# Attention beside a token MLP: score banks as two groups of three, VectorE's tiles in a group's last bank, the schedule's table replaced

## Chip, cores and metric

One core of one Trainium2 chip runs the whole program. The metric is the device time in microseconds (us) of one execution; lower is better. Runs of the kernel before: 757.68, 756.87, 756.53 and 756.96 us, median 756.91.

## What is computed

The input x has 2048 tokens of 640 features. A layer norm feeds two branches, and their product is added to x.

```python
xn = _layernorm(x)                       # (1, 2048, 640)
# branch A: 32 heads of 20 features, all 2048 keys, then wo
scores = einsum("bhqd,bhkd->bhqk", q, k) * (20 ** -0.5)
o = einsum("bhqk,bhkd->bhqd", softmax(scores), v)
s = merge_heads(o) @ wo
# branch B: an MLP over the tokens, on a layer norm of xn
u = gelu(einsum("bsd,sf->bdf", h, w1) + b1)      # w1 2048x1536
g = silu(einsum("bdf,fs->bds", u, w2) + b2)      # w2 1536x2048
out = x + s * g
```

The costly part is the softmax: 32 x 2048 x 2048 exponentials.

## The kernel before, in words

**Units.** Heads are taken in 8 groups of four, queries in 4 blocks of 512: 32 passes. In a pass there are 16 chunks of 128 keys and four heads, so 64 units (pass, chunk, head): a unit is one score tile of 128 keys by 512 queries, one PSUM bank of 512 floats, 2048 units in all. The four heads of a group sit in the four 32-row groups of TensorE (PE), so score matmuls of different heads run side by side (`emit_st`, the matmul of L1212).

**Two engines make exponentials.** ScalarE (ACT) takes neighbouring banks in one instruction (`emit_exp`, L1241): an exp of two units (128x1024, a "pair") or of three (128x1536, a "triple"), written to `pt_sb`. VectorE (DVE) takes its units by a bit trick: one instruction per unit from PSUM to 16-bit integers (`emit_op1`, L1252, tiles `dt_sb`), and three instructions per four units that add constants (`emit_top`, L1276). The four results are combined in the following matmuls with scaled values. DVE's units come from five chunks in a pass (`RC`), at most; the planner decides as it goes. Then the PV matmuls (`pv_mm`, L1292) multiply by the values and accumulate a pass in bank 6 (`AB`), and DVE finishes the pass (L1408 and after).

**Banks.** PSUM has eight. ACT's units go to `ACT_GROUPS = ((0, 1, 2), (3, 4))`, taken in turn: while ACT reads one group, PE fills the other. Bank 5 (`DB`) holds a unit for DVE and nothing else, once the start is over; bank 6 is the accumulator; bank 7 (`JB`) serves every other job that needs a bank (projections, MLP) and, when free, DVE (`SHARE`). A group of three may *lend* its last bank: the set of score matmuls then gives ACT a pair and DVE the third bank (`do_st`). That is done when DVE has less than `LEND` ns of work waiting in the planner's account.

**Other work.** The projections, the values, both MLP halves (L645) and the output projection (L930) are PE jobs put between the sets; their evacuations are on DVE, some at the start on ACT (L1044, L1047). All DMAs are issued by SyncE (SP) in one order. Weights of the MLP come in parts of 1 MB and 768 KB, two parts at a time in `regA` (L775, L782).

**What sets the order.** `schedule` is a planner that runs while the program is built: it holds a clock per engine and a cost per instruction, picks the next instruction, and so writes a fixed order for each engine, with semaphore waits where data or banks cross engines. Its options are switched every 16 units by a table, `PLAN`: a row has one digit for each entry of `OPTS` and picks one of that option's values (`tune`). The start, in which the layer norm, the transposes and the first projections feed the first passes, is called ramp in the code; in it all free banks serve jobs until the first score tile is due (`withdraw`). A job that holds a bank of a group keeps the group from being filled (`fin_bank`). At the end the banks of the score ring become `tbank`, in which the output projection of the last four token blocks is begun before the last pass is done (`tail_pre`).

Of the kernel before, what the change touches and what calls it, by code (L numbers as in the profile page):

```python
# [260 lines left out]
class _Kern:  # L261
# [4 lines left out]
    NG = 8  # L266
    EPS = 1e-5
    RP = 20
    ACT_GROUPS = ((0, 1, 2), (3, 4))
    DB = 5  # L270
    AB = 6
    JB = 7
    RC = (2, 5, 8, 11, 14)
# [12 lines left out]
    CONFL = True  # L286
    FILL, FGAP, FACT = True, 40.0, 0.6
    LATE = 2.0
    LEND, LEND_MIN = 1100.0, 3
    SHARE = True  # L290
    VPRIO = 24.0
    QAT = (0.0, 0.0, 0.0, 0.0)
# [10 lines left out]
        ("MINJ", (640.0, 320.0, 1000.0)),  # L303
        ("ROOM", (3, 6, 0)),
        ("DRIDE", (400.0, 150.0, 700.0)),
        ("LEND", (900.0, 300.0, 1500.0, 0.0, 2500.0)),
        ("PARTS", ((2,), (2, 1), (3, 1), (1,), ())),
        ("LATE", (2.0, -9.0, 99.0)),
        ("DON", (True, False)),
# [5 lines left out]
        ("GROT", (1, 0)),  # L315
    )
    PLAN = (
        "00000000000010", "00000000000000", "00000000000010", "00000000000000", "00000410000000", "10010410000100",
        "00004010011000", "20204010111000", "00000000000000", "02000020010010", "00000000000000", "00000010001000",
        "00000000000000", "01000120000000", "01003120000000", "00000000000000", "00000010000100", "00000310100000",  # L320
        "02020320011000", "02020320011000", "02120010011000", "00000220000100", "30000220000100", "02000010000000",
        "00000000000000", "00000000100000", "02000100100100", "01000120001010", "00000000000000", "00003300000000",
        "00000000000000", "01000000000010", "00004000000000", "10011000000000", "01022300000000", "00000000000000",
        "30020100000000", "02000010110000", "00000100000000", "00010100000110", "00001000000000", "20100000000100",
        "11000000000000", "00000000000000", "00001000010000", "10020000000000", "10020000010000", "10020010010000",
        "00000000000000", "22103000000000", "22103010000000", "01220100000100", "00000000000000", "00100000001000",
        "02000000100000", "01000300001000", "01000300001000", "00000000000000", "00100000001000", "00100400100000",
        "01000000001000", "00004000000000", "10002000010000", "01001400001010", "01021420000110", "00000300000000",
        "00000020000010", "00000000000000", "00000010001000", "10000100000000", "10000100000000", "10004100001000",
        "00004120000000", "00001010000000", "10011410000110", "11001200000110", "11001200100110", "00020000000000",  # L330
        "00000000000000", "00000000100100", "00200400100000", "02100010110010", "02101010100010", "01000000000000",
        "01000000000000", "00000000000000", "00000400000000", "00000000000000", "00000020001000", "00020320000000",
        "00000000000000", "01000010000000", "01000010000100", "20000000000100", "02000000000000", "12000000000000",
        "00001000101000", "00000000000000", "00200000010100", "00020020100000", "01003000000000", "22000000000000",
        "21210000000000", "00000000000000", "00200020110000", "00000000000000", "00200000000100", "00000000001000",
        "00020310000100", "00220020000010", "10224000000010", "31223410000010", "30200000000100", "00021000000010",
        "00100000001010", "01100000010010", "01204001000000", "01204100001000", "00204100000010", "02024120000000",
        "02024320000000", "02000200000000", "12000200010000", "00000000000000", "00001000100000", "00001000100000",
        "00000000001000", "10000000000000", "00000000000000",
    )  # L340
    PARTS = (2,)
    DX = (1, 2, 3)
# [74 lines left out]
    def schedule(self):  # L417
        pr, t, nc = self.prog, self.t, self.nc
        S, NB, NTB, F, FC, D, H, DH, NG, GH = (self.S, self.NB, self.NTB, self.F, self.FC, self.D,
                                               self.H, self.DH, self.NG, self.GH)  # L420
# [11 lines left out]
        PROW = 4096  # L432
        A_x, A_wqkv, A_wo, B_w1, B_b1, B_w2, B_b2, out = (self.A_x, self.A_wqkv, self.A_wo, self.B_w1,
                                                          self.B_b1, self.B_w2, self.B_b2, self.out)
        AB, DB, JB = self.AB, self.DB, self.JB
        RC, NR = self.RC, len(self.RC)
        sl = {}

# [11 lines left out]
        done = set()  # L450
# [320 lines left out]
        def dma_w1(k):  # L771
            src = B_w1[:, k * 256:(k + 1) * 256].rearrange("(b p) f -> p b f", p=P)
            dst = w1_ap(k)
            wr = [S_(f"wm{k % 2}")]
            return ("dma", lambda e: e.dma_start(dst, src), [], wr, f"dma_w1_{k}", S * 512,  # L775
                    [S_(f"x{b}") for b in range(NB)] if k < 2 else [])

        def dma_w2(k):
            src = B_w2[:, k * 256:(k + 1) * 256].rearrange("(fc p) s -> p fc s", p=P)
            dst = w2_ap(k)  # L780
            wr = [S_(f"wn{k % 2}")]
            return ("dma", lambda e: e.dma_start(dst, src), [], wr, f"dma_w2_{k}", F * 512,  # L782
                    [S_("wm0"), S_("wm1")] if k < 2 else [])

        def ztmp(i):
# [181 lines left out]

        jobs = []
        bankq = []
        freebanks = [3, 4, DB, 0, 1, 2, JB]  # L970
        retired = set()
        busybanks = set()
        active = []
# [85 lines left out]
        dquads = []  # L1059
        tfree = list(range(self.NTILE))  # L1060
        dlive = [0]
        dbank = ["free"]
        dop1 = []
        lent = set()
        dtop = []
# [97 lines left out]
        def d_bank():  # L1163
            if not dveready[0]:
                return None
            if DB in bank_off:
                return None
            if dbank[0] == "free" and fin_bank(DB):
                return DB
            if self.SHARE and JB in freebanks and len(dop1) < 2 and not ramp[0]:  # L1170
                return JB
            return None

        def d_take(g, bk):
            d = d_cur[0]
            if d is None:
                q, c, r = d_claimable()
                claimed.add((q, c))
                dlive[0] += 1
                d = d_cur[0] = dict(q=q, c=c, r=r, todo=[0, 1, 2, 3], tl=[tfree.pop(0), None, None, None], fin=[0.0] * 4, left=4, pk=0)  # L1180
                stats["dve_units"] += 4
                nd_pass[q] += 1
            d["todo"].remove(g)
            if bk == DB:
                dbank[0] = "full"
            elif bk == JB:
                freebanks.remove(bk)
                busybanks.add(bk)
            else:
                lent.add(bk)  # L1190
            dop1.append((d, g, bk))
            u = (d["q"], d["c"], g)
            if not d["todo"]:
                d_cur[0] = None
            return u
# [52 lines left out]
        def emit_op1():  # L1248
            d, g, bk = dop1.pop(0)
            w = dt_sb[:, d["tl"][0], g, :]  # L1250
            src = ps(bk)
            tk = pr.dve(lambda e: e.tensor_scalar(w, src, WOFF, 0.0, ALU.add, ALU.max), reads=[bank_slot[bk]],  # L1252
                   writes=[S_(f"dt{d['tl'][0]}_{g}")], name=f"dw{d['q']}_{d['c']}_{g}", cost=601.0)
            if bk == DB:
                dbank[0] = "free"
            elif bk != JB:
                lent.discard(bk)
            else:
                busybanks.discard(bk)
                freebanks.append(bk)  # L1260
                freebanks.sort(reverse=True)
            d["left"] -= 1
            if d["left"] == 0:
                dtop.append([d, 1])
                d["fin"][0] = tk.fin
                if self.EARLY:
                    dquads.append((0.0, d))
# [170 lines left out]
        for i, (b0, nb) in enumerate(LN):  # L1438
            rq = () if i < 4 else (f"xn{LN[i - 1][0] + LN[i - 1][1] - 1}",)
            steps = ln_steps(b0, nb)  # L1440
            k = next(n for n, x in enumerate(steps) if x == ("tag", f"lnp{b0}")) + 1
# [16 lines left out]
        for w in (1, 0):  # L1458
            src = A_wqkv[:, 640 * w + 256:640 * w + 640].rearrange("(kc p) f -> p kc f", p=P)
# [196 lines left out]
        def withdraw(bs):  # L1656
            for b in bs:
                retired.add(b)
                if b in freebanks:
                    freebanks.remove(b)  # L1660

        def fin_bank(b):
            return b not in busybanks
# [273 lines left out]
        while True:  # L1937
# [6 lines left out]
                ramp[0] = False  # L1944
            if not dveready[0] and "qk0_1_3" in done:
                dveready[0] = True
                withdraw([DB])
            nomore = next_chunk(a_cur[0], claimed) is None and a_cur[1] is None
            if nomore:
                for b in act_banks:  # L1950
# [3 lines left out]
                            done.add(f"tbank{len(tbank)}")  # L1954
                            tbank.append(b)
            if (nomore or (a_cur[0] == NP - 1 and a_left(NP - 1) < self.D_GUARD)) and d_cur[0] is None and not dop1:
                if DB not in bank_off:
                    bank_off.add(DB)
                    done.add(f"tbank{len(tbank)}")
                    tbank.append(DB)  # L1960
                if not bankq and JB not in busybanks and JB not in bank_off:
                    bank_off.add(JB)
                    done.add(f"bankoff{JB}")
# [61 lines left out]
```

The softmax here doesn't subtract the row's maximum and nothing guards it: scores larger than these inputs give would overflow.

## Time and profile before

The page shows one execution of 757.68 us, whose span from the first to the last instruction is 755.9 us, at a granted TensorE clock of 0.999.

| what | value |
|---|---|
| run of the profile, its span | 757.68 us, 755.9 us |
| busy PE, DVE, ACT | 726.7, 718.3, 731.3 us |
| exps on ACT (L1241) | 662: 434 pairs and 228 triples |
| units on DVE (L1252) | 496 of 2048 |
| first exp starts, last exp ends | 14.07 us, 745.2 us |
| ACT busy from 45.0 to 745.2 us | 697.9 of 700.2 us |

How to read it: busy is the time in which an engine has an instruction running, as a union of records. A record of ACT or DVE reaches a little into the next one, so small delays do not show as idle. A "pitch" below is the step from the start of one record to the start of the next on the same engine. The chain of waits is followed back from the last instruction, at each step to what released it.

### The profile page before, as it was taken

To read this page: it belongs to the slowest core of one execution; us is meant where nothing else is said; L and a number is where in the kernel's file an instruction comes from. 1 tells how busy PE (TensorE), PEld (TensorE's weight loads), DVE (VectorE), ACT (ScalarE), POOL (GpSimd) and SP (SyncE) were. 2 spreads that over 40 slices of the span, in tenths; PEclk is the share of its full clock that TensorE was granted. 3 is DMA by queue.
4 is the path that set the end of the run, shared out by engine and by line. 5 is a ranking of instruction groups with operands and counts; after the bars stand their busy time and mean duration, and the time that the engine had idled before them with its cause. 6 is when DMAs were issued, how large, how long until landed. Compare 5 with 4: busy or idle time off the path is not lost.

```text
span 755.9 us, 22917 instructions
## 1 busy us (share of the span) xinstructions
PE 726.7 (96%) x10194; PEld 246.7 (33%) x10194; DVE 718.3 (95%) x1319; ACT 731.3 (97%) x686; POOL 15.7 (2%) x22
## 2 busy tenths in 40 slices
PE   8899999999999999999999989999999999999997
PEld 6332233322332323323232233333333333322232
DVE  7799999999999999999999999999999898999996
ACT  4999999999999999999999999999999999999994
POOL 4200000000000000000000000000000000000001
PEclk9999999999999999999999999999999999999999
DMA  8684111101130302203010131331133410410002
GB/s 240 94 161 84 40 20 37 21 13 30 37 63 12 76 13 45 61 26 76 13 39 13 37 91 31 68 81 28 44 82 69 112 48 2 152 47 30 30 13 70
DMA packets 117143, 42.54 MB, mean 56 GB/s; under 512 B 75300, under 2 KB 115876, under 8 KB 116996
## 3 DMA queue, kind: packets, MB, share of 16 engines
q1 hardware_dynamic: 117044, 41.07, 23.4%
q8 instruction: 80, 1.31, 0.7%
q14 instruction: 19, 0.16, 0.1%
HBM read 26.37 MB, written 10.22 MB: 48 GB/s over the span
## 4 chain that ended last, share of the span: by engine, by line
ACT 67%; PE 23%; SPq 4%; DVE 3%; DMA 3%; POOL 1%; issue 0%; DVEq 0%; ACTq 0%
ACT pt_sb L1241 65%; PE ps_all L1212 7%; PE ps_all L1292 7%; PE ps_all L645 7%; SPq L906 3%; DMA xnT_sb<-regC 1%; PE ps_all L930 1%; ACT zt_sb L836 1%; DMA regA<-in_B_w_dram 1%; DMA wqk_sb<-in_A_wqkv_dram 1%; DVE dt_sb L1252 1%; PE ps_all L630 1%; SPq L1425 0%; POOL st_sb L567 0%; DVE v_sb L1045 0%
## 5 line engine op out<-in xcount | busy, mean ns | idle before, releaser
L1241 ACT ACTIVATE pt_sb<-ps_all 128x1024 bf16<-128x1024 f32 (+1 forms) x662 | 711.5, 1213 | 3.4 <-PE ps_all L1212 2.4
L1252 DVE TENSOR_SCALAR dt_sb<-ps_all 128x512 uint16<-128x512 f32 x496 | 330.1, 680 | 16.9 <-PE ps_all L1212 15.4
L1212 PE MATMUL ps_all<-qk_sb 32*128 32x512 bf16 x2048 | 286.6, 384 | 18.9 <-ACT pt_sb L1241 14.8
L1276 DVE TENSOR_SCALAR dt_sb<-dt_sb 128x2048 uint16<-128x2048 uint16 x372 | 245.4, 682 | 1.6
L1212 PEld LDWEIGHTS ps_all<-qk_sb 32*128 32x128 bf16 x2048 | 73.8, 91 | 276.7 <-ACT pt_sb L1241 193.3
L1292 PE MATMUL ps_all<-pt_sb,v_sb 128*21 128x512 bf16 x1552 | 123.6, 382 | 1.0 <-DVE v_sb L1045 1.0
L1292 PE MATMUL ps_all<-dt_sb,vs_sb 128*21 128x512 bf16 x1488 | 123.6, 381 | 0.3 <-DVE dt_sb L1276 0.2
L645 PE MATMUL ps_all<-regB,regA 128*32 128x128 bf16 (+1 forms) x1536 | 66.8, 301 | 1.2 <-DMA regA<-in_B_w_dram 0.9
L645 PE MATMUL ps_all<-regC,regA 128*32 128x512 bf16 (+1 forms) x1536 | 65.7, 301 | 0.0
L1292 PE MATMUL ps_all<-dt_sb,v_sb 128*21 128x512 bf16 x496 | 48.9, 384 | 0.5 <-DVE tr_sb L1408 0.3
L645 PE MATMUL ps_all<-xnT_sb,wqk_sb 128*32 128x512 bf16 x640 | 48.9, 382 | 0.3 <-DVE v_sb L1045 0.2
L1292 PEld LDWEIGHTS ps_all<-pt_sb,v_sb 128*21 128x21 bf16 x1552 | 29.1, 90 | 50.5 <-issue 38.5
L1292 PEld LDWEIGHTS ps_all<-dt_sb,vs_sb 128*21 128x21 bf16 x1488 | 31.6, 91 | 38.2 <-issue 18.4
L645 PEld LDWEIGHTS ps_all<-regB,regA 128*32 128x32 bf16 x1536 | 28.1, 96 | 28.2 <-issue 12.1
L645 PEld LDWEIGHTS ps_all<-regC,regA 128*32 128x32 bf16 x1536 | 28.4, 96 | 25.6 <-issue 11.7
L930 PE MATMUL ps_all<-wv_sb,xnT_sb 128*128 128x128 bf16 (+3 forms) x160 | 30.1, 302 | 0.1
L645 PE MATMUL ps_all<-wv_sb,xnT_sb 128*32 128x480 bf16 x320 | 23.6, 369 | 0.2 <-DVE v_sb L1045 0.2
L1408 DVE STREAM_TRANSPOSE tr_sb<-ps_all 128x512 f32<-128x512 f32 x31 | 21.9, 705 | 0.0
L645 PEld LDWEIGHTS ps_all<-xnT_sb,wqk_sb 128*32 128x32 bf16 x640 | 14.3, 95 | 20.0 <-issue 8.7
L1292 PEld LDWEIGHTS ps_all<-dt_sb,v_sb 128*21 128x21 bf16 x496 | 12.4, 90 | 23.6 <-issue 18.1
L815 DVE TENSOR_SCALAR zt_sb<-ps_all,b2h_sb 128x512 bf16<-128x512 f32 (+1 forms) x32 | 17.2, 542 | 1.4 <-PE ps_all L645 1.2
L1045 DVE CAST v_sb<-ps_all 128x480 bf16<-128x480 f32 (+1 forms) x24 | 14.2, 593 | 2.3 <-PE ps_all L738 2.1
(81 smaller groups left out, 291.9 us busy)
## 6 DMA issues: line engine op xcount, KB each, us to landing
regA<-in_B_w_dram SPq DMA_DIRECT2D x6, 1024.0 KB
regA<-in_B_w_dram SPq DMA_DIRECT2D x8, 768.0 KB
qk_sb<-qk_scratch_dram SPq DMA_DIRECT2D x56, 80.0 KB
qk_scratch_dram<-qs_sb SPq DMA_DIRECT2D x32, 128.0 KB
regA<-in_A_x_dram SPq DMA_DIRECT2D x6, 640.0 KB
ok_scratch_dram<-on_sb SPq DMA_DIRECT2D x96, 20.0 KB
out_dram<-regC SPq DMA_DIRECT2D x3, 640.0 KB
wqk_sb<-in_A_wqkv_dram SPq DMA_DIRECT2D x2, 480.0 KB
```

The source lines that it names most:

```text
L630: steps.append(("pe", lambda e, dc=dc, lhsT=lhsT: e.matmul(ps(bk, n), lhsT, xnT_sb[:, dc, tb * 512 + c0:tb * 512 + c0 + n], start=(dc == 0 ...
L645: fns.append(lambda e, c=c, e_=e_: e.matmul(oc(c, e_), lhsT[:, c:e_], rhs, start=start, stop=stop, tile_position=(0, c)))
L815: steps.append(("dve", lambda e, z=z, i=i, jj=jj: e.tensor_scalar(z[:, c0:c0 + n], ps(bk, n, i * n), 0.5, bias[:, jj:jj + 1], ALU.mult, AL ...
L906: steps.append(("dma", lambda e, d=d, src=src: e.dma_start_transpose(d, src), [S_(f"okd{pass_of[(G, tb)]}_{g}") for G in range(L6) for g i ...
L930: steps.append(("pe", lambda e, c=c, k=k: e.matmul(ap, oT_sb[0:k, c, b * 128:(b + 1) * 128], wo_ap[0:k, c, c0:c0 + n], start=(opens and c ...
L1045: return lambda e: e.tensor_copy(dst, src)
L1212: pr.pe(lambda e, outp=outp, lhsT=lhsT, rhs=rhs, g=g: e.matmul(outp, lhsT, rhs, start=True, stop=True, tile_position=(32 * g, 0)), reads=[ ...
L1241: tk = pr.act(lambda e: e.activation(outp, inp, AF.Exp, scale=math.log(2.0) / 128.0), reads=[bank_slot[b] for b in banks[:n]], writes=[S_( ...
L1252: tk = pr.dve(lambda e: e.tensor_scalar(w, src, WOFF, 0.0, ALU.add, ALU.max), reads=[bank_slot[bk]], writes=[S_(f"dt{d['tl'][0]}_{g}")], n ...
L1276: tk = pr.dve(lambda e: e.tensor_scalar(dst, src, dk, None, ALU.add), reads=[S_(f"dt{b0}_{g}") for g in range(4)], writes=[S_(f"dt{b}_{g}" ...
L1292: pr.pe(lambda e: e.matmul(outp, lhsT, rhs, start=(k == 0), stop=last, tile_position=(0, 32 * g)), reads=reads, writes=[bank_slot[AB]], na ...
L1408: steps.append(("dve", lambda e: e.transpose(tr_sb[:, :], ps(AB)), [bank_slot[AB]], [S_("tr")], f"epT{q}", 632.0))
```

## The change

`ACT_GROUPS` becomes two groups of three, banks 0 to 2 and 3 to 5. `DB` goes, with all code that treated it: DVE's units now come from the last bank of either group, lent as before, or from `JB`. `LEND` is raised (1100 to 1800 ns, and its table values to 1800, 1300, 2400, 700 and 0). In the planner's account a part of `w1` or `w2` now costs 1.8 times as much DMA time. All 129 rows of `PLAN` are new. No instruction is of a new kind. As the planner decides the order, each engine's whole order changes: the built program has 464 pairs and 208 triples (672 exps), again 496 units and 372 additions on DVE, and the same matmuls but for the fillers that keep the array busy (176 against 100 zero matmuls at L1307, 101 against 69 warm-up matmuls at L1317).

```diff
-    ACT_GROUPS = ((0, 1, 2), (3, 4))
-    DB = 5
+    ACT_GROUPS = ((0, 1, 2), (3, 4, 5))
...
-    LEND, LEND_MIN = 1100.0, 3
+    LEND, LEND_MIN = 1800.0, 3
...
-        ("LEND", (900.0, 300.0, 1500.0, 0.0, 2500.0)),
+        ("LEND", (1800.0, 1300.0, 2400.0, 700.0, 0.0)),
...
     PLAN = (
...
-            return ("dma", lambda e: e.dma_start(dst, src), [], wr, f"dma_w1_{k}", S * 512,
+            return ("dma", lambda e: e.dma_start(dst, src), [], wr, f"dma_w1_{k}", S * 922,
...
-            return ("dma", lambda e: e.dma_start(dst, src), [], wr, f"dma_w2_{k}", F * 512,
+            return ("dma", lambda e: e.dma_start(dst, src), [], wr, f"dma_w2_{k}", F * 922,
...
-        freebanks = [3, 4, DB, 0, 1, 2, JB]
+        freebanks = [3, 4, 5, 0, 1, 2, JB]
...
-            if DB in bank_off:
+            if JB in bank_off:
                 return None
-            if dbank[0] == "free" and fin_bank(DB):
-                return DB
             if self.SHARE and JB in freebanks and len(dop1) < 2 and not ramp[0]:
                 return JB
...
-            if bk == DB:
-                dbank[0] = "full"
-            elif bk == JB:
+            if bk == JB:
...
                 dveready[0] = True
-                withdraw([DB])
...
-                if DB not in bank_off:
-                    bank_off.add(DB)
-                    done.add(f"tbank{len(tbank)}")
-                    tbank.append(DB)
```

More of the change, by code (lines that the diff above doesn't have):

```diff
@@ L317 @@
     PLAN = (
[L318 to L337, printed above, removed]
@@ L338 @@
-        "02024320000000", "02000200000000", "12000200010000", "00000000000000", "00001000100000", "00001000100000",
-        "00000000001000", "10000000000000", "00000000000000",
+        "00000000000010", "00000000000000", "00100000001000", "00000000000000", "10200300000100", "10200300100100",
+        "20020000000010", "20022010000010", "10000000000100", "00000100000000", "01000100000100", "00000000000000",
+        "20102000000000", "00000000000000", "00000000010000", "01000300010000", "01002310100110", "01010300110000",
@@ new lines @@
+        "01010320100000", "01021310100000", "01001310000100", "10000200010000", "10022210011000", "11022220011000",
+        "00103300000010", "00102300000010", "21102000000000", "00000200000010", "20200000000000", "10201000000000",
+        "10000200010000", "12000000010000", "00000000000000", "01000000000100", "01022300000100", "00022300010100",
+        "02000010000010", "00000000000000", "00200010100010", "00000010110010", "01003000000100", "01000200010100",
+        "01000200010100", "10000000100000", "10000010100100", "10100010000100", "01010020011100", "00000000000000",
@@ new lines @@
+        "01000200000000", "00000000000000", "00010000110000", "01010010110000", "21010310111000", "22110310111010",
+        "00003100001000", "01000000000100", "01000000101100", "01010000101100", "00000000000000", "10000000010100",
+        "01000000001110", "00000000001100", "00000000000000", "00001000000000", "22020000000000", "00000000000000",
+        "01000000100000", "02000010100000", "01000010100000", "00000000000000", "01000300000000", "11020300000100",
+        "11020300000000", "11120100000000", "11120100000010", "11120100010110", "11210100011110", "12210100011110",
@@ new lines @@
+        "02210100011010", "11210100001010", "11221100011010", "11201100111010", "11201210111110", "10020420000000",
+        "00000000000000", "02000001010000", "30000000011000", "00000420000000", "00000400000100", "00100000100000",
+        "01000200000000", "01000200000000", "00000000000000", "00023000101000", "01000000001000", "00100000000100",
+        "00000000000000", "00000020000000", "00000000000000", "00001010000010", "01100000000000", "10000000000000",
+        "00000000000000", "00000020100000", "10002320100000", "10200010001000", "10202010001000", "01200110011100",
@@ L340 @@
+        "00002000100000", "02002000010000", "00022020010000", "00000000000000", "00001001010100", "00001000111100",
+        "00010420000000", "02001000001100", "00000000000000", "20000000100000", "00000300000000", "00104310000000",
+        "00000100100010", "10020100100010", "30000100100010", "00002000001000", "01012000000000", "00000000000000",
+        "00000320000000", "00022310000000", "00022311000000",
     )
@@ L434, in schedule @@
                                                           self.B_b1, self.B_w2, self.B_b2, self.out)
-        AB, DB, JB = self.AB, self.DB, self.JB
+        AB, JB = self.AB, self.JB
         RC, NR = self.RC, len(self.RC)
@@ L1061, in schedule @@
         dlive = [0]
-        dbank = ["free"]
         dop1 = []
@@ L1253, in emit_op1 @@
                    writes=[S_(f"dt{d['tl'][0]}_{g}")], name=f"dw{d['q']}_{d['c']}_{g}", cost=601.0)
-            if bk == DB:
-                dbank[0] = "free"
-            elif bk != JB:
+            if bk != JB:
                 lent.discard(bk)
```

## Prediction

> **What bounds the kernel.** I read the busy shares first, then ACT by slices, then the chain by engine.
>
> ```profile
> PE 726.7 (96%) x10194; PEld 246.7 (33%) x10194; DVE 718.3 (95%) x1319; ACT 731.3 (97%) x686; POOL 15.7 (2%) x22
> ...
> ACT  4999999999999999999999999999999999999994
> ...
> ACT 67%; PE 23%; SPq 4%; DVE 3%; DMA 3%; POOL 1%; issue 0%; DVEq 0%; ACTq 0%
> ```
>
> Three engines are nearly full, but only ACT is full in every slice save the first and last, and it holds 67% of the chain. The windows (PE, PEld, DVE, ACT, POOL busy, then clock, DMA share, GB/s), cut at the first exp, the end of the ramp and the last exp, tell the same:
>
> ```profile
> 0.00:14.07 14.07, 12.62 (x107) 10.56 (x108) 11.04 (x37) 4.25 (x7) 7.00 (x14) 1.00 0.87 277
> 14.07:45.00 30.93, 27.76 (x252) 12.35 (x251) 25.50 (x87) 29.15 (x29) 5.76 (x5) 1.00 0.67 113
> 45.00:745.20 700.20, 679.77 (x9810) 221.62 (x9809) 674.74 (x1181) 697.87 (x653) 0.63 (x1) 1.00 0.21 49
> 745.20:755.90 10.70, 6.55 (x32) 2.13 (x30) 6.98 (x16) 0.01 (x1) 2.27 (x2) 0.94 0.18 63
> ```
>
> Between 45 and 745 us ACT is idle for 700.2 - 697.9 = 2.3 us, PE for 20.4, DVE for 25.5. The time is therefore: when ACT starts, what it has to do, how often it is late, and the tail.
>
> How much is lateness? The exps by form (busy, mean record | idle before):
>
> ```profile
> L1241 ACT ACTIVATE pt_sb<-ps_all 128x1024 bf16<-128x1024 f32 x434 | 435.2, 1066 | 1.0 <-PE ps_all L1212 0.6
> L1241 ACT ACTIVATE pt_sb<-ps_all 128x1536 bf16<-128x1536 f32 x228 | 340.4, 1493 | 2.4 <-PE ps_all L1212 1.8 <-PE ps_all L1292 0.3
> ```
>
> The records overlap, so I take pitches from the starts of single records: undisturbed, a pair steps 0.916 us and a triple 1.343. 434 x 0.916 + 228 x 1.343 = 703.7 us; all exps together are busy for 711.5 (line L1241), so 7.8 us are delays hidden in the overlap, and 3.4 (1.0 + 2.4) are visible: 11 us of lateness in all. Some 3 us of it lie in the ramp. So ACT's lateness after 45 us, **about 7.5 us, is all that a better order of the main part can win**: 1% of the run.
>
> **The change part by part.** I count from the built order of each engine and price with rows of before.
>
> *Number of exps.* 672 exps for the same 1552 ACT units (464 pairs, 208 triples): 464 x 0.916 + 208 x 1.343 = 704.4, **+0.7 us**. The Trainium skill ("ScalarE: Activation LUTs", rules for kernel authors) budgets about 0.3 us per ACTIVATE plus 0.83 ns per element, which speaks against more and smaller exps. The slope agrees here ((1493 - 1066)/512 = 0.834 ns), the fixed part does not: 3 x 0.916 - 2 x 1.343 = 0.06 us for an instruction in a stream. By the rule 10 more would cost an estimated 3.0 us, by the row 0.6. The row decides, being this stream.
>
> *First exp.* Before, the first score set goes to banks 3 and 4 while the first value projections use other banks. After, all six banks belong to groups, and in PE's order 20 value matmuls (128x160) stand ahead of the first set, which waits for ACT: ACT evacuates both value tiles itself before its first exp. PE is free for them at about 13.6 us, where the first set stood. Eight such matmuls hold PE for 0.54 to 0.57 us in before's timeline: 20 take 1.45, to 15.1. ACT's evacuation of 320 columns: between its rows of 256 (0.38) and 384 (0.49) stands 0.44. Then 0.06 for the semaphore, 0.39 for the set and 0.06 again: first exp at 16.1 against 14.07, **+2.1**.
>
> *Ramp.* ACT's timeline of before (start, length, brackets: idle before and releaser):
>
> ```profile
> 21.15 5.54 ACT L1241 ACTIVATE pt_sb<-ps_all 128x1024 bf16<-128x1024 f32 x5 [0.20 <-PE ps_all L1212]
> 26.54 0.64 ACT L1047 ACTIVATE qk_sb<-ps_all 128x512 bf16<-128x512 f32 x1
> 27.02 4.68 ACT L1241 ACTIVATE pt_sb<-ps_all 128x1536 bf16<-128x1536 f32 x4
> 32.55 4.62 ACT L1241 ACTIVATE pt_sb<-ps_all 128x1536 bf16<-128x1536 f32 x4 [0.84 <-PE ps_all L1212]
> 37.03 0.63 ACT L1047 ACTIVATE qk_sb<-ps_all 128x512 bf16<-128x512 f32 x1
> 38.24 0.38 ACT L1044 ACTIVATE qk_sb<-ps_all 128x256 bf16<-128x256 f32 x1 [0.58 <-PE ps_all L630]
> 38.79 0.39 ACT L1044 ACTIVATE qk_sb<-ps_all 128x256 bf16<-128x256 f32 x1 [0.16 <-PE ps_all L630]
> ```
>
> Two of 512 columns (0.48 each by pitch) and one of 256 (0.28) move to DVE, which idles for 5.4 us in this window: **-1.25**. The brackets sum to 1.8 us of waiting for keys. After, ACT comes 2 us later and DVE has fewer value evacuations ahead of its layer norm, so transposes are asked for earlier; two waits remain by the order: the first key part must be evacuated on ACT after the third exp (about 0.45), and at the change to the second pass the set for the next exp stands on PE behind PV matmuls that need the exp before it (0.06 + 0.16 + 0.11 + 0.39 + 0.06, 0.8). 1.25 against 1.8: **-0.5**. DVE's first unit is later (after the first pass's finish, at about 50 us against 39.95) but its work before is longer too; by pitches it is some 5 us behind at 50 us. That lies under its 25.5 us of idle time; with that cover gone it would delay lent banks.
>
> *One late weight part.* Before, SP issues a part of w2 only after 16 transposes, and PE waits:
>
> ```profile
> 593.38 1.26 SPq L906
> ...
> 594.74 5.76 DMA regA<-in_B_w_dram
> ...
> 602.44 0.35 PE ps_all L1212 x3
> ```
>
> ACT loses 1.0 us there (waits of 585 to 606 us: 1.0, once). In the new order all w2 parts are issued ahead of these transposes: **-1.0**. Next to be late are the transposes, needed only for the output projection 50 us on.
>
> *Refills.* This is the undecided term. A set of scores must be filled while ACT reads the other group: 0.916 us beside a pair. The chain where PE sets the pace:
>
> ```profile
> 101.39 0.32 PE ps_all L645 x4
> 101.70 0.43 PE ps_all L1292 x8
> 102.14 0.20 PE ps_all L645 x4
> 102.34 0.32 PE ps_all L1212 x3
> 102.66 0.33 PE ps_all L1292 x4
> ```
>
> Four PV or projection matmuls cost 0.22 and any change between scores and these 0.11 more (0.33 against 0.22). The skill ("TensorEngine Tiling (Array Packing)", key properties) says a change of tiling mode drains TensorE, which speaks against this change: PE's order has 625 runs of scores against 591, 68 more mode changes, 68 x 0.11 = 7.5 us; yet runs that need two rounds become fewer (four or more scores: 72 against 178), at 0.11 to 0.22 each 12 to 23 us back, less 34 more first rounds of 0.22 (7.5). In total PE gains or loses a few us. But it is spread otherwise: with these rates PE's load per 128 units reaches 45 us at units 512 to 640 (42 before), where ACT has 46; in the stretches with MLP or projections PE had 87 to 96% of ACT's work before and has 92 to 98% after.
>
> I laid PE's work between any two refills against the exps between them (rates above, 0.5 us for semaphores and the set). Where PE has more, ACT must wait: these overhangs sum to 7.7 us in before's order, near its 7.5 measured, and to 7.9 in after's. The same for DVE, a lent bank's reading against the refill two sets later, gives 1.0 before and nothing after. By the overhangs the term is +0.2; if lateness follows density instead (0.2 us per 45 us at 88% load, 0.5 near 93%, 0.8 at 95.6%, single stretches of before), it is +2.7. Bounds: -6 (no lateness left) and +7 (doubled). I take **+0.7**, nearer the direct count.
>
> *Tail.* With no `DB` to hand over early, 20 instead of 17 wide output matmuls follow the last PV: 3 x 0.27 = 0.8, half of it under DVE's queue of evacuations: **+0.5** (0 to 0.8).
>
> Sum: 0.7 + 2.1 - 1.25 - 0.5 - 1.0 + 0.7 + 0.5 = **+1.3**. On the profiled span: 757.2, its run 757.68 + 1.3 = 759.0. That run is 0.8 above the median of the runs, so the forecast for the median is 756.9 + 1.3 = **758.2 us**.
>
> **Rivals.**
> 1. *Density decides (slower).* Where PE stands near 96% of ACT's work or higher (six stretches of 45 us), one late wait for a lent bank stops PE in its order, and ACT with it. For: 14.8 us of PE waiting for ACT in before show how tight the handover is. Against: before lives with 95.6% in one stretch. Price 1 us per such stretch or more: +3.5 to +8, 760.5 to 765.
> 2. *Lateness falls (faster).* Both groups are alike, and every unit of DVE rides in a set that is filled anyway. If the 6.5 us of lateness left fall below 4, the sum turns negative: 752 to 755.4. Price: at 2 us left, 756.9 + 0.6 - 4.5 = 753. It decides from about 2 us less lateness. Below 751 there is nothing to win, for ACT's work does not shrink.
> 3. *It does nothing that counts* since DVE's tiles waited in PE's queue before as well (469 score matmuls wait for DVE before, 455 after): part of the forecast's own case.
>
> **Chances.** Forecast with rival 3 (756 to 760): 0.45. Rival 1: 0.28. Rival 2: 0.27. A change of 0.2% (1.5 us) is about what this measurement can tell from none. The forecast's case splits 0.04 faster, 0.22 same, 0.19 slower. Together 0.31, 0.22, 0.47. The range reaches from rival 2's better half to past rival 1: 752 to 766; the forecast's own is 756 to 760.
>
> **What would show it.** First exp at about 16 us with two value evacuations ahead; 672 exps, pitches still 0.916 and 1.343; no wait for weights near 600; ACT idle from 45 us on near 2 us visible. Wrong if a pair's pitch changes, if DVE's late start shows as gaps of ACT after 50 us, if units 512 to 640 take over 48 us (44.9 before), or if weight parts come late elsewhere.

## Result and the profile after

The changed kernel takes **755.78 us** (median of 43 runs, 755.38 to 757.65), the one before 757.01 beside it (64 runs). The ratio is 0.9984, with a 95% interval of 0.9978 to 0.9989: about 1.2 us faster. The forecast said 758.2, 1.3 us slower. Its range held the time; its sign did not hold.

The page of the changed kernel, span 753.9 us (755.9 before), has these three lines: busy shares, ACT by slices, and the chain by engine.

```profile
PE 717.6 (95%) x10302; PEld 240.6 (32%) x10302; DVE 720.8 (96%) x1320; ACT 729.8 (97%) x695; POOL 15.7 (2%) x22
...
ACT  4999999999999999999999999999999999999993
...
ACT 85%; PE 12%; DVE 2%; DMA 1%; issue 0%; POOL 0%
```

ACT still bounds the kernel, now with 85% of the chain instead of 67%; PE's part of it fell from 23 to 12%, and SP's 4% are gone. PE, which was to become tighter, is busy for 9 us less. The windows, cut again at the first exp, 45 us and the last exp:

```profile
0.00:15.59 15.59, 14.33 (x136) 12.22 (x136) 11.91 (x41) 5.12 (x8) 7.70 (x15) 1.00 0.94 272
15.59:45.00 29.41, 26.04 (x267) 12.28 (x267) 22.60 (x81) 28.70 (x22) 5.06 (x4) 1.00 0.75 156
45.00:742.44 697.44, 669.51 (x9865) 213.38 (x9862) 679.63 (x1183) 695.94 (x665) 0.63 (x1) 1.00 0.21 47
742.44:753.90 11.46, 7.71 (x47) 2.72 (x43) 6.62 (x16) 0.00 (x0) 2.26 (x2) 1.00 0.16 57
```

The first exp starts 1.5 us later, the last ends 2.8 us earlier, and the tail is 0.8 us longer. Idle time of ACT in the long stretch fell only from 2.3 to 1.5 us (697.44 - 695.94); most of what was won lies in delays that the overlapping records hide, as the prediction warned. The exps by form (busy, mean record | idle before):

```profile
L1235 ACT ACTIVATE pt_sb<-ps_all 128x1024 bf16<-128x1024 f32 x464 | 450.3, 1086 | 0.5 <-PE ps_all L1206 0.2
L1235 ACT ACTIVATE pt_sb<-ps_all 128x1536 bf16<-128x1536 f32 x208 | 300.8, 1526 | 1.9 <-PE ps_all L1206 1.8
```

The counts are those of the built order. The mean records grew by 20 and 33 ns (1066 and 1493 before), which is no slower exp: the commonest steps from one exp to the next are the same in both traces (0.904 us behind a pair, 1.331 behind a triple). In the changed kernel the six pairs before which ACT visibly waits (over 0.02 us) have records of 1024 ns in the mean, the others 1088: a record without a wait before it reaches into the exp ahead. So a **longer** mean record at the same pitch says that sets are ready earlier.

Summing each exp's step over the prediction's pitches (0.916 and 1.343 us) gives ACT's lateness: from 50 us on it is 7.4 us before and 4.7 after. These pitches lie 0.012 us above the commonest steps. Over 0.904 and 1.331 the sums would be 14.7 and 12.1 us. The difference of some 2.7 us does not hang on this choice; the level does. Lateness in what follows is the sum over the prediction's pitches, good for differences between kernels. With that the difference of the two spans can be laid beside the prediction's terms:

| term | predicted | read from the two traces |
|---|---|---|
| start to 46 us (first exp +2.1, evictions -1.25, waits -0.5) | +0.35 | -0.65: exps worth 28.8 us done by 46 us, 28.2 before |
| ten more exps | +0.7 | +0.6 (30 more pairs, 20 fewer triples) |
| late weight part | -1.0 | -1.1 |
| refills | +0.7 | **-1.6** (7.4 - 4.7 less the weight part) |
| tail | +0.5 | +0.8 |
| sum | +1.3 | -1.9 (spans: -2.0) |

One profiled execution against one: that is 0.7 to 0.8 us more than the medians differ (1.2), and no trace says in which term the excess lies. Of the terms that missed, only the refills are 2.3 us off, enough to turn the sign alone; the start, 1.0 us off, is not.

### The profile page after: what moved, and what is told of

Its sections match the earlier page's. It is cut to its first block, busy times and chain, and to the rows that moved or that the text cites. A ratio compares the mean times of both kernels' runs of the same rounds, so it can differ in the third digit from the quotient of the medians.

```text
span 753.9 us, 23158 instructions
## 1 busy us (share of the span) xinstructions
PE 717.6 (95%) x10302; PEld 240.6 (32%) x10302; DVE 720.8 (96%) x1320; ACT 729.8 (97%) x695; POOL 15.7 (2%) x22
## 4 chain that ended last, share of the span: by engine, by line
ACT 85%; PE 12%; DVE 2%; DMA 1%; issue 0%; POOL 0%
ACT pt_sb L1235 83%; PE ps_all L1284 4%; PE ps_all L644 4%; PE ps_all L1206 4%; ACT zt_sb L840 1%; ACT zt_sb L835 1%; PE ps_all L929 1%; DMA xnT_sb<-regC 1%; DVE bst_sb L531 0%; DVE bst_sb L533 0%; DMA regA<-in_A_x_dram 0%; DVE regC L549 0%; DVE regC L1607 0%; PE ps_all L683 0%; DVE xnT_sb L611 0%
## 5 line engine op out<-in xcount | busy, mean ns | idle before, releaser
L1246 DVE TENSOR_SCALAR dt_sb<-ps_all 128x512 uint16<-128x512 f32 x496 | 326.6, 680 | 10.3 <-PE ps_all L1206 8.4
L1206 PE MATMUL ps_all<-qk_sb 32*128 32x512 bf16 x2048 | 266.7, 384 | 27.7 <-ACT pt_sb L1235 24.8
L1268 DVE TENSOR_SCALAR dt_sb<-dt_sb 128x2048 uint16<-128x2048 uint16 x372 | 240.7, 682 | 1.4
L1206 PEld LDWEIGHTS ps_all<-qk_sb 32*128 32x128 bf16 x2048 | 66.9, 91 | 283.9 <-ACT pt_sb L1235 231.7
L644 PE MATMUL ps_all<-regC,regA 128*32 128x512 bf16 (+1 forms) x1536 | 68.4, 301 | 0.0
L1044 DVE CAST v_sb<-ps_all 128x480 bf16<-128x480 f32 (+1 forms) x22 | 13.3, 607 | 3.3 <-PE ps_all L737 3.1
```

Source lines behind the costliest of these rows:

```text
L644: fns.append(lambda e, c=c, e_=e_: e.matmul(oc(c, e_), lhsT[:, c:e_], rhs, start=start, stop=stop, tile_position=(0, c)))
L1044: return lambda e: e.tensor_copy(dst, src)
L1206: pr.pe(lambda e, outp=outp, lhsT=lhsT, rhs=rhs, g=g: e.matmul(outp, lhsT, rhs, start=True, stop=True, tile_position=(32 * g, 0)), reads=[ ...
L1268: tk = pr.dve(lambda e: e.tensor_scalar(dst, src, dk, None, ALU.add), reads=[S_(f"dt{b0}_{g}") for g in range(4)], writes=[S_(f"dt{b}_{g}" ...
```

## Experiments

Two ideas stood against each other. **Count**: ACT is late only where PE's work between two refills exceeds the exps between them (the "overhangs"). **Density**: lateness follows PE's load. The prediction took a value between them. My count charged a run of six scores (two sets back to back) with its second round of 0.22 us for both sets. Charging only the second set changes the sums from 7.7 and 7.9 us (before, after) to 6.3 and 5.2. This mended count was made with the result known, so it has to forecast something new.

**1. Load without overhang, overhang without more load.** The changed kernel with 60 groups of four zero matmuls more on PE; in the first run at the roomiest places, in the second at the tightest.

```diff
             self.schedule()
+            self.pad()
             pr.final_waits()
...
+            if i in self.PADS:
+                for g in range(4):
...
+                        outp, zw_sb[:, 0:DH + 1], wp_sb[:, 0:2, :, :], start=False, stop=False,
```

> The changed kernel with 60 extra groups of four zero matmuls on PE (0.216 us each, 13.0 us in all), each put at a place where PE's work up to the next refills leaves the most room under the exps. PE's busy share between 50 and 745 us rises from 96.0% to about 98%. Count theory (ACT is late only where PE has more work between two refills than the exps between them take): the overhangs stay at 5.2 us, so the time stays that of the changed kernel, ratio to before 0.998 to 0.9995. Density theory (lateness follows PE's load, as rival 1 and the upper bound of the prediction had it): 3 to 7 us more than the changed kernel, ratio 1.002 to 1.008.

> The changed kernel with the same 60 groups of zero matmuls (13.0 us), now put where the room is smallest. Count theory: the overhangs rise from 5.2 to 13.3 us, so 8 us more than the changed kernel (6 to 9), ratio to before 1.006 to 1.011. Density theory: the same as with the pads at the roomy places, 3 to 7 us, ratio 1.002 to 1.008.

Measured: roomy 757.95 us, ratio 1.001 [1.0001, 1.0019], some 2 us over the changed kernel's ratio of 0.9984; tight 764.89 us, ratio 1.0105 [1.0091, 1.0119], some 9 us over it. The same window of 100 to 740 us (PE, PEld, DVE, ACT, POOL busy and instructions), first of the changed kernel, then roomy, then tight:

```profile
100.00:740.00 640.00, 614.54 (x9157) 196.89 (x9150) 626.47 (x1091) 639.34 (x613) 0.63 (x1) 1.00 0.20 47
```

```profile
100.00:740.00 640.00, 620.97 (x9347) 199.50 (x9339) 625.45 (x1089) 639.14 (x612) 0.63 (x1) 1.00 0.20 47
```

```profile
100.00:740.00 640.00, 617.52 (x9306) 199.72 (x9294) 620.33 (x1077) 635.52 (x605) 0.63 (x1) 1.00 0.19 46
```

In the roomy run PE does 190 matmuls more in these 640 us and ACT loses one instruction; in the tight run PE does fewer extra matmuls, and ACT falls 8 instructions behind. Lateness from 100 us on is 4.4, 5.3 and 12.5 us: +0.9 for 48 pads (10.4 us of PE's time) where there is room, +8.1 for 57 pads where there is none, against 8.1 counted. The other 12 roomy pads stand ahead of 100 us, partly among the first 30 exps, which the count leaves out, and there ACT lost 1.3 us. So the time of PE's work alone costs ACT little: its place does. The tight run fell where the count had put it. The roomy run fell between the two forecasts: 2 us over the changed kernel are less than density's 3 to 7, but more than the count allowed. Density falls as the main explanation, not to nothing: of 2 us, 0.9 were not counted, and the loss at the start was outside the count.

**2. When is the first set of six ready?** No kernel is needed for this; where ACT visibly waits, the trace tells. The changed kernel near 227 us, PE and then ACT (start, length, brackets: idle before):

```profile
226.07 0.60 PE L1284 MATMUL ps_all<-pt_sb,v_sb 128*21 128x512 bf16 x8
226.60 0.71 PE L1206 MATMUL ps_all<-qk_sb 32*128 32x512 bf16 x6
227.24 0.61 PE L1284 MATMUL ps_all<-dt_sb,vs_sb 128*21 128x512 bf16 x8
```

```profile
222.62 4.24 ACT L1235 ACTIVATE pt_sb<-ps_all 128x1536 bf16<-128x1536 f32 x4
227.03 3.28 ACT L1235 ACTIVATE pt_sb<-ps_all 128x1024 bf16<-128x1024 f32 x3 [0.17 <-PE ps_all L1206]
```

Six scores start at 226.60 and occupy PE until 227.31, but the exp that waits for them starts at 227.03, 0.43 us after the first of them. All five exps that wait ahead of a run of six start 0.43 to 0.44 us after it, the same as most of those ahead of a run of three. The second round is in nobody's way but the next set's.

**3. Banks or table?** Four kernels cross them: the old and the new banks, each without a table (all options at their defaults), and each with the other's table and `LEND` values.

```diff
-    PLAN = (
-        "00000000000010", "00000000000000", "00000000000010", "00000000000000", "00000410000000", "10010410000100",
...
+    PLAN = ()
```

> The banks as before (three, two, and one for VectorE), but no table: every option at its default, the same defaults as in the next run. ACT's exps by pitch 3.6 us more from the 40th exp on (488 units on DVE instead of 496), overhangs of PE's work 10.9 us against 6.3 in before, tail +0.9 or 0. Count theory: 7 to 9 us over before, ratio 1.010 to 1.012. Density theory (PE's total work is nearly that of before): 3.6 us over before, ratio 1.005.

> Two groups of three banks, no table, the same defaults. Overhangs 7.2 us, ACT's exps by pitch 3.6 us over the changed kernel (488 units on DVE). Theory A (the banks themselves lower the lateness, by the count): 3 to 4 us less than the run with the old banks and no table, so 4.5 to 5.5 us over before, ratio 1.006 to 1.0075. Theory B (only the new table does it, the banks cost the later first exp, more exps and a longer tail): the same as or slower than the old banks without a table, ratio 1.010 to 1.014.

> Two groups of three banks with the old table and the old LEND values. The planner then gives DVE 420 units instead of 496; ACT's exps by pitch are 31 to 32 us longer, overhangs 9.1 us. Count theory: about 34 us over before, near 791 us. If the table mattered little (only the banks): within 5 us of the changed kernel.

> The old banks with the new table and the new LEND values. 508 units on DVE, ACT's exps by pitch 4 us shorter than before, but overhangs 9.8 (PE) and 4.9 us (DVE) and, more than these, five of the eight w2 parts issued by SP behind the 16 transposes. If late weight parts stop PE as the one of before did: tens of us over before, 790 to 815 us. If they are hidden (the count alone): about 3 us over before, near 760 us.

Measured: old banks without table 766.11 us, ratio 1.0117 [1.0103, 1.0131]; new banks without table 763.57, ratio 1.0086 [1.0072, 1.01]; new banks with the old table 792.86 (one run); old banks with the new table 813.77 (one run). Without a table, then, the new banks are worth 2.5 us by themselves, less than the 3 to 4 counted, and the ratio lies between the two forecasts: lateness from 50 us on is 11.4 against 9.3 us where the overhangs said 10.9 and 7.2. The rest of the step from 9.3 to 4.7 is the new table's. The old table in the new banks gives 420 units to DVE, and the extra exps cost what pitches say they cost. The new table in the old banks lets five of the eight w2 parts be issued behind the transposes: the last exp ends at 751.3 us there, two tanh instructions of the MLP after it wait for 5.4 and 8.2 us, and the span is 812.0. A table belongs to the banks that it was searched for. (The third part of the change, 922 in place of 512 in the account of the weights, has no share: with 512 the new banks and table give the same order on every engine.)

**4. The late weight part alone.** The kernel before, with one DMA moved in SP's order, on a semaphore of its own.

```diff
             self.schedule()
+            self.early_w2()
...
+        m = [x for x in sp if x.name == "dma_w2_6"][0]
+        tr = [x for x in sp if x.name.startswith("oTt")]
...
+        sp.remove(m)
+        sp.insert(sp.index(tr[0]), m)
```

> The kernel before with one DMA moved: SP issues the late w2 part ahead of the 16 transposes instead of behind them; nothing else changes. Theory (weights): PE no longer waits near 600 us, ACT keeps the 1.0 us it lost there; the time falls by 0.7 to 1.2 us (ratio to before 0.9984 to 0.9991) and ACT's lateness between 550 and 650 us falls from 2.0 to about 1.0 us. Rival (hidden anyway): the transposes, now later, or the next refill take the 1.0 us over; ratio 1.000. Rival (the whole gain is this DMA): ratio 0.9975 or lower.

Measured: 756.36 us, ratio 0.999 [0.9982, 0.9999]. SP's queue in that run:

```profile
568.47 3.16 SPq L1450 DMA_DIRECT2D ok_scratch_dram<-on_sb  x4
571.68 0.49 SPq L807 DMA_DIRECT2D regA<-in_B_w_dram  x1
572.22 25.08 SPq L931 DMA_TRANSPOSE xnT_sb<-ok_scratch_dram  x16
```

The weights are issued at 571.7 us instead of 594.7. ACT's lateness between 600 and 650 us falls from 1.64 to 0.55 us, and no other 50 us stretch after the start moves by more than 0.02: the 1.0 us of the prediction, with nothing late in its place. The interval of the time excludes, narrowly, that the move is worth nothing, and it excludes the rival's 0.9975. It does not exclude the changed kernel's own 0.9984, so by the times alone this one DMA could be most or all of the 1.2 us. That the main part won more besides is read from the traces: lateness falls by 2.7 us with the change, by 1.1 with this DMA alone.

**5. The first exp.** The changed kernel with another order in which jobs take banks, so that one group is free when the first scores are due.

```diff
-                    freebanks.sort(reverse=True)
+                    freebanks.sort(key=(JB, 2, 1, 0, 5, 4, 3).index)
```

> The changed kernel with another order in which jobs take banks at the start: the second value job takes bank 2 and not 5, so the group of banks 3 to 5 is free when the first scores are due. PE issues the first set ahead of the 20 value matmuls; the order from the third pass on stays as it is. Both theories: first exp near 14 us instead of 15.6 (on this start of the weights). Theory A (the start of ACT counts, the prediction's +2.1): the time falls by 1.3 to 2 us below the changed kernel, ratio to before 0.9955 to 0.997. Theory B (keys, which depend on the layer norm, the transposes and DVE, set the end of the ramp): ACT waits for keys later and gives it back; within 0.5 us of the changed kernel, ratio 0.998 to 0.999.

Measured: 756.62 us, ratio 0.9995 [0.9984, 1.0005]: no faster than the changed kernel, by the ratios some 0.8 us slower, though the intervals overlap. ACT at the start, first in the changed kernel, then in this one:

```profile
13.99 0.44 ACT L1043 ACTIVATE v_sb<-ps_all 128x320 bf16<-128x320 f32 x1 [0.41 <-PE ps_all L737]
14.68 0.44 ACT L1043 ACTIVATE v_sb<-ps_all 128x320 bf16<-128x320 f32 x1 [0.25 <-PE ps_all L737]
15.59 4.14 ACT L1235 ACTIVATE pt_sb<-ps_all 128x1536 bf16<-128x1536 f32 x3 [0.48 <-PE ps_all L1206]
20.00 0.38 ACT L1043 ACTIVATE qk_sb<-ps_all 128x256 bf16<-128x256 f32 x1 [0.27 <-PE ps_all L629]
20.28 24.28 ACT L1235 ACTIVATE pt_sb<-ps_all 128x1536 bf16<-128x1536 f32 x18
45.38 2.79 ACT L1235 ACTIVATE pt_sb<-ps_all 128x1536 bf16<-128x1536 f32 x2 [0.82 <-PE ps_all L1206]
```

```profile
14.14 1.45 ACT L1235 ACTIVATE pt_sb<-ps_all 128x1536 bf16<-128x1536 f32 x1
15.63 0.44 ACT L1043 ACTIVATE v_sb<-ps_all 128x320 bf16<-128x320 f32 x1
16.54 27.10 ACT L1235 ACTIVATE pt_sb<-ps_all 128x1536 bf16<-128x1536 f32 x20 [0.48 <-PE ps_all L1206]
44.36 0.60 ACT L1046 ACTIVATE qk_sb<-ps_all 128x512 bf16<-128x512 f32 x1 [0.72 <-PE ps_all L629]
45.44 2.79 ACT L1235 ACTIVATE pt_sb<-ps_all 128x1536 bf16<-128x1536 f32 x2 [0.49 <-PE ps_all L1206]
```

The first exp is 1.45 us earlier, and the last two triples before the second pass start at 45.4 us in both. What is gained at 14 us is lost at the change of pass, where ACT takes over a query evacuation and waits for it. 28.8 us of exps are done by 46 us in either. Most of the 0.7 us by which this profile's span is longer arises later, between 200 and 250 us, where lateness is 0.9 us instead of 0.4; why was not found out.

**6. A table made for the count.** If overhangs are the lateness, a table searched for few overhangs should win.

> The changed kernel with another table, found by a search for the smallest sum of the planner's start (first 40 exps), ACT's exps by pitch from there on, the overhangs and the tail; the banks, the options and the first 40 exps stay. 673 exps, 496 units on DVE as before; overhangs 1.8 us instead of 5.2, tail 0.9 us shorter, ACT's exps by pitch the same. Count theory: 3 to 4 us less than the changed kernel, ratio to before 0.993 to 0.9945; lateness of ACT from 50 us on about 2 us instead of 4.7. Rival (the count is right only on the average, its errors are as large as what is left, so a table that fits it wins little): 0 to 1.5 us less than the changed kernel, ratio 0.9965 to 0.9985. Rival (the planner's own clock, which puts this order 1.5 us later than the changed kernel's): ratio 1.000 or above.

Measured: 755.68 us, ratio 0.998 [0.9969, 0.9991], the same as the changed kernel; lateness from 50 us on is 4.8 us, not 2. It is spread otherwise: 0.5 us in all between 350 and 650 us (1.4 in the changed kernel), but 1.1 from 250 to 300 and 1.2 from 700 on. The largest of PE's waits from 50 to 742 us (us in total, times, longest; waits shorter than some 0.2 us do not show), in the changed kernel and then here:

```profile
PE ps_all L1206 <- ACT pt_sb L1235: 21.8, 60, 0.9
PE ps_all L1284 <- DVE tr_sb L1400: 0.9, 2, 0.6
PE ps_all L1284 <- DVE dt_sb L1268: 0.7, 3, 0.3
PE ps_all L644 <- DVE zt_sb L814: 0.4, 2, 0.2
```

```profile
PE ps_all L1206 <- ACT pt_sb L1235: 15.8, 52, 1.1
PE ps_all L1284 <- DVE tr_sb L1400: 1.5, 4, 0.6
PE ps_all L1284 <- DVE dt_sb L1268: 1.3, 6, 0.2
PE ps_all L644 <- DVE zt_sb L814: 0.9, 4, 0.3
PE ps_all L929 <- DVE regC L944: 0.6, 2, 0.3
```

PE's waits for DVE, smaller ones included, doubled from 2.5 to 4.9 us in all. The count has PE's work in it and not PE's waiting, so the search may well have moved the loss to where the count is blind; how much of the loss these waits make was not measured. For instance PE waits 0.39 us for DVE's `tr_sb` until 274.58 us; the set behind it starts at 275.56, and its exp, at 275.99, is 0.4 us late. The first of the two rivals came true: the count tells a bad order from a good one, not a good one from a better one.

**7. A table made with all three engines, and the clock.** The next table was searched on a replay that also has PE's waits for DVE.

> The changed kernel with a third table, searched on a replay of all three engines' orders from the 40th exp on: pitches of the traces of before and of the changed kernel, each wait for PE, ACT or DVE in its place, and three latencies set so that the replay meets the stretch from the 40th exp to the last in seven of the profiles within 1.5 us. Unlike the count it contains PE's waits for DVE. It puts this order 1.2 us ahead of the changed kernel's up to the last exp and 0.6 us more in the tail, and the order of the previous run (the table made for the count) 0.5 us behind up to the last exp. Theory (the count's blind spot was PE's waiting for DVE): 1 to 2 us less than the changed kernel, ratio to before 0.9955 to 0.997. Rival (what is left is below what such a model resolves): as the changed kernel, 0.9978 to 0.9989.

Measured: 756.32 us, ratio 0.9991 [0.9981, 1.0001], no gain. From 50 to 700 us lateness did fall, to 3.1 us (4.0 in the changed kernel), but from 700 us on it is 1.7 us instead of 0.7. The windows of this run (PE, PEld, DVE, ACT, POOL, clock, DMA share, GB/s):

```profile
692.00:696.00 4.00, 3.26 (x48) 0.97 (x44) 3.39 (x7) 4.00 (x4) 0.00 (x0) 1.00 0.00 0
696.00:700.00 4.00, 2.86 (x35) 0.70 (x27) 3.96 (x7) 4.00 (x5) 0.00 (x0) 0.98 0.02 4
700.00:704.00 4.00, 3.98 (x35) 0.94 (x31) 4.00 (x9) 3.19 (x3) 0.00 (x0) 0.60 0.00 0
```

After a stretch in which PE had less to do, the granted clock is 0.60 over 4 us (0.50 from 700 to 702). PE is then busy throughout, and ACT loses 0.8 us visibly in the last window. Five of its eleven runs have a mean clock of 0.998 (median 755.6 us), six of 0.994 or 0.995 (756.7). The search had left out the planner's own guard against such stretches. So the last kernel adds seven groups of zero matmuls to this order, in the manner of experiment 1:

```diff
+    PADS = {9188: 1, 9192: 1, 9774: 2, 9814: 3}
```

> The order of the previous run with seven groups of four zero matmuls more on PE: five between 693 and 698 us, where PE had little to do ahead of the stretch of 700 to 704 us in which the trace granted half the TensorE clock, and two near 633 us. Theory (too little work on PE lets the clock go, and that hid the gain): the clock stays at 1.00 from 700 to 704 us, ACT's lateness from 700 us on falls from 1.7 to about 0.8 us, no run shows a mean clock under 0.998, and the time falls by 0.9 to 1.4 us, ratio to before 0.997 to 0.9985. Rival (the clock falls for another reason): half the clock again, ratio 0.999 to 1.000.

```profile
692.00:696.00 4.00, 3.60 (x56) 1.05 (x52) 3.92 (x7) 4.00 (x5) 0.00 (x0) 1.00 0.02 4
696.00:700.00 4.00, 3.62 (x47) 1.03 (x43) 3.40 (x7) 4.00 (x5) 0.00 (x0) 1.00 0.00 0
700.00:704.00 4.00, 3.73 (x46) 1.03 (x47) 4.00 (x9) 4.00 (x4) 0.00 (x0) 1.00 0.00 0
```

Measured: **754.87 us**, ratio 0.9978 [0.9969, 0.9988]; the clock stays at 1.00, and lateness from 700 us on is 0.7 us. More work on PE made the kernel faster: by 1.0 us by the ratios (0.9991 to 0.9978), as much as the lateness fell; the medians differ by 1.4, but of this 0.25 is a difference between the runs of before beside them. The two intervals overlap; the clock in the profiles and in the runs (0.998 or more in all ten) tells them apart more clearly than the time. This is the fastest median here, 1.6 us under before and perhaps 0.5 under the changed kernel, whose interval overlaps with it.

## Why the prediction was wrong

**The refills (+0.7; in truth about -1.6)** are the step that failed. Its direct count had the right idea and one wrong charge, the second round of a run of six put on both sets; it made 7.7 of 6.3 us before and 7.9 of 5.2 after. So the term came to +0.2 where the mended count gives -1.1, and with -1.1 the whole sum would have been some 0.5 us faster. The remaining 0.5 us to the -1.6 of the traces is not accounted for. Experiment 2 shows the charge wrong, experiment 1 confirms the mended count for work added at tight places, experiment 3 its order of kernels with errors up to 2 us. That 7.7 lay near the 7.5 "measured" was luck: the level of lateness depends on the pitch taken. Over the steps that the trace shows most often, 0.904 and 1.331 us, it is twice as much, so 7.5 us is not shown to be all that a better order can win. And it held the 1.1 us of the late weight part, which a count of PE's work does not contain. Taking +0.7, a step towards the density figure of +2.7, added to it: a fear of 95.6% load that the pads show to be worth little. The stretch that it was to hurt first, units 512 to 640, took 46.9 us, under the mark of 48, and ACT's lateness between 200 and 250 us, where these units lie, fell from 0.76 to 0.38 us. The gain needs no mechanism beyond those the prediction had; it named this as rival 2. That rival's own mark, lateness under 4 us, was not reached: less the weight part, lateness fell by 1.6 us, and 4.7 are left. The mark was set too low, for the other terms sum to +0.55, so a refill term below -0.55 turns the sign.

**First exp (+2.1), evictions (-1.25) and waits (-0.5)**, in sum +0.35, came out as -0.65. The first exp itself was nearly right (15.59 us; an estimate of 16.1 if ACT's first evacuation, at 12.43 us here, came as late as in before, at 12.90). What was wrong was adding it: experiment 5 shows that the start of ACT is not on the path to the end of the start phase. It is the change of pass that is.

**Right in size:** ten more exps at +0.7 (the unrounded sums give 0.63), by the row of 0.06 us for an exp in a stream (0.05 by the commonest steps); the late weight part, -1.0 against -1.1, shown alone in the trace of experiment 4; the tail, +0.5 against +0.8. The wait of 0.8 us at the change of pass stands in the trace as 0.82.

**Open:** why the overhangs of the new banks are smaller with equal options (7.2 against 10.9 us) was not taken apart further. Sets of three that need one round speak for it (in before and the changed kernel, runs of four or more scores fall from 178 to 72); no run isolates them.

## What to carry to other kernels

Where one engine bounds and another feeds it through a few buffers, lay the feeder's work between two refills against the consumer's work between them, and charge each set only with what stands ahead of it; the feeder's average load said little here even at 96%. Such a count is good for sorting orders and finding the 10 us ones, but a search that is fed with it can find its blind spots, here, it seems, the feeder's own waits for a third engine. And before adding a later start to a sum, look for the next point where the engine waits for something else: here, up to there, an earlier start was worth nothing.

## What was not expected of the hardware

Seven small groups of work that computes nothing, 1.5 us of PE's time, bought about 1 us: without them TensorE's granted clock fell to half for 3.4 us. Little work alone does not decide it. In the changed kernel PE is busy for 2.86 us of 696 to 700 us too, as in experiment 7, and in experiment 6 for only 2.45 us of 612 to 616 us; the clock stays at 1.00 behind both. It fell in two runs of experiment 3, to 0.64 over 4 us behind a stretch with 2.12 us of work (new banks, old table, at 604 us) and to 0.62 behind one with 1.68 (old banks, new table, at 476 us). What else it takes is open.

The start moves by itself by almost 1 us. ACT's table load, which waits for the first weights, starts at 7.8 to 8.9 us in the profiles here. In the changed kernel the fourth exp waits for a key part, for which PE waits on a DMA transpose (`xnT_sb<-regC`); PE goes on at 18.8 us in its profile and at 19.7 in that of experiment 6, with the same transposes issued from 13.3 us on. Differences of less than 1 us between two single profiles are therefore read stretch by stretch, not from the spans.
